# Expert and SwiGLU stage: two up products in a row, then the down products of both

## The chip, the cores and the metric

The program runs on one core of a Trainium2 chip. TensorE multiplies matrices into PSUM; VectorE (DVE), ScalarE (ACT) and GpSimd (POOL) do the element-wise work; SyncE (SP) issues the transfers. The metric is the device time of one execution in microseconds. Before the change three runs took 2143.82, 2144.63 and 2146.75 us, so the median is 2144.63.

## The reference

Attention with a local or a strided mask, a mixture of eight experts whose token weights come from Sinkhorn iterations, and a SwiGLU block with RMS norm, all in float32:

```
attn = softmax(where(mask, q k^T / sqrt(64), -1e9)) v          # 4 x 8 heads x 576 x 64
x    = attn as 2304 tokens x 512
P    = exp(x w_gate - max);  8 times: rows / sum, columns / sum, * N / E
moe  = sum over e of P[:, e] * (relu(x w1[e]) w2[e])           # 8 experts, 512 -> 1024 -> 512
xn   = moe / sqrt(mean(moe^2) + 1e-6) * rms_g
out  = (silu(xn w_gate2) * (xn w_val)) w_out                   # 512 -> 1536 -> 512
```

## The kernel before

Attention and expert 0 come first and take about 330 us of the span. The change lies in what follows: experts 1 to 7 and the SwiGLU block (three passes over its hidden columns, treated as groups 8 to 10). The tokens are cut in three thirds of 768. A *visit* is one group on one third; the list `quads` holds the 21 visits of experts and the 9 of SwiGLU in order.

A visit consists of *rounds*: four for an expert, two for a SwiGLU pass. Each matrix is split into a high and a low part, and a product of two such matrices is three matmuls (high by high, high by low, low by high). The up side uses a scheme of seven block products (`PROD`, line 839) in place of eight. One entry of `PROD` is a `product` (line 1016): six matmuls of 384 columns into one of two PSUM banks, `ub0` and `ub1`. The tuple's third number says which bank, the fourth whether the bank starts anew:

```
PROD = [(0, 0, 0, True), (1, 1, 1, True), (4, 4, 0, False), (3, 3, 1, True),
        (5, 5, 0, False), (6, 2, 1, False), (2, 6, 0, False)]
```

An expert round runs these seven once. A SwiGLU round runs them twice, for the gate and then for the value, fourteen products in all. The banks swap roles after each seven (`turn_u`).

`outcome(i, a, b, use)` (line 1041) issues what reads a product out. For products 0, 2 and 3 it is a ScalarE copy (line 1047). For products 1, 4 and 5 of an expert it is a VectorE addition (line 1062), then relu on ScalarE (line 1036) and on VectorE the low part of the hidden block (line 1037). For product 6 relu and the low part read the bank directly. SwiGLU has a sigmoid (1073) and multiplications (1074, 1084), with additions in 1071 and 1082. A bank may be written again only when its reader is done; a product that accumulates waits for that reader too.

A *down* (`down_one`, line 1437) is three matmuls of 512 columns (lines 701 to 703) from a hidden block of the round before into one of six PSUM banks `db0` to `db5`. A round has twelve of them (`downs`, line 1420). In the first round of a visit the downs of the visit before come to their end, and `evict` (line 1454) issues a VectorE instruction for each of the six banks (line 1460 for experts, 1471 for SwiGLU). Such a round is called an eviction round in what follows.

What decides the order: the loop over products (line 1558) issues a product, its outcome and one step of the background clock (`bg.pump`), then as many downs as the list `upto` (line 1514) allows after this product, each with a step of that clock. Each engine runs its instructions in the order of issue. Background work hangs on that clock: the conversion of the SwiGLU weights on VectorE (`convert`, lines 805 to 826), the splitting of the next weights (`combine`, lines 856 to 863, and `prepare_2`, lines 934 and 937 on ScalarE and GpSimd), loads and stores. Three rounds in which tiles are transposed for the norm take `upto` from the table `TURNS` (line 1492). In the first visit `columns_1` (line 687) writes column sums into the free part of a product bank, which line 691 reads.

Of the kernel before, what the change touches and what calls it, by code (L numbers as in the profile page):

```python
# [92 lines left out]
def kernel(  # L93
# [595 lines left out]
    def columns_2(area, ps):  # L689
        c = area[:, NTILE + E : NTILE + 2 * E]  # L690
        nc.vector.tensor_scalar(out=c, in0=ps, scalar1=1e-9, scalar2=None, op0=ALU.add)
        nc.vector.reciprocal(out=c, in_=c)
        nc.vector.tensor_tensor(
            out=prob, in0=prob, in1=c[:, None, :].to_broadcast([P, NTILE, E]), op=ALU.mult
        )
        nc.vector.tensor_scalar(out=prob, in0=prob, scalar1=float(NT) / E, scalar2=None, op0=ALU.mult)
# [467 lines left out]
    with tc.manual_schedule():  # L1164
# [117 lines left out]
        for g in range(1, len(groups)):  # L1282
            due = SL * (first[g] // TA) - 4 * (LOOK + (PRE if groups[g][0] else 0)) - DUE
            steps = [step for t in ticks[last[g - 1] + 1 : last[g] + 1] for step in t]
# [62 lines left out]
        for idx in range(-LOOK, n1 - LOOK):  # L1347
# [8 lines left out]
            if u.f == 0:  # L1356
                if "x" not in u.cell:
                    fetch(u)
                if u.left:
                    bg.add(gate(u.t0, u.n, u.cell["x"]), 20)  # L1360
                    if u.at:
                        area = fa[:, :1280], fa[:, 1280:3328].bitcast(F32R)
                        steps = sums(0, us[0].cell["x"], *area) if u.at == 1 else []
                        steps += sums(u.at, u.cell["x"], *area)
                        bg.add(steps, 30 if u.at == 1 else SUMS, tag="sums")
                else:
# [5 lines left out]
                    steps = []  # L1372
# [17 lines left out]
            if not u.left and u.f == 0:  # L1390
                begin_psum()
                place = db[4], db[5], acc[:, 0], wgc2
                steps = []
# [26 lines left out]
        def downs(r):  # L1420

            n, j, hs = r
            g, qd, _ = quads[n]
            last_j = NF // 2 - 1 if g < E else NG // 2 - 1
            half = NF // 2 if g < E else NG // 2
            order = (1, 2, 3, 0) if j == 0 else (0, 1, 2, 3)
            seen = set()
            out = []
            for i in order:
                f = j + (half if i in (2, 3) else 0)  # L1430
                for t in range(3):
                    b = t + (3 if i in (1, 2) else 0)
                    out.append((r, i, t, b, f, j == 0 and b not in seen, j == last_j and b in seen))
                    seen.add(b)
            return out
# [61 lines left out]
        for n, (g, qd, ends_group) in enumerate(quads):  # L1497
# [10 lines left out]
            for j in range(rounds):  # L1508
                chains = [j] if g < E else [2 * j, 2 * j + 1]
                steps = 7 * len(chains)  # L1510
                hs = [4 * ((hround + 1) % 2) + i for i in range(4)]
                hround += 1
                todo = downs(done) if done is not None else rest
                upto = [len(todo) * (i + 1) / steps for i in range(steps)]
                turns = {}
                if turning is not None:
                    at, upto = TURNS[steps]
# [31 lines left out]
                for ci, s in enumerate(chains):  # L1549
# [8 lines left out]
                    for i, (wk, xk, which, begins) in enumerate(PROD):  # L1558
# [16 lines left out]
                        if n == 0 and i in (1, 6):  # L1575
# [4 lines left out]
                            steps = [lambda to=free_part: columns_2(totals, to)]  # L1580
# [61 lines left out]
```

## Time and profile before

| | |
|---|---|
| median of three runs | 2144.63 us |
| the profiled execution | 2145.55 us, of which the span of instructions 2143.7 us |
| TensorE matmul | 2086.0 us, 97% of the span, 11343 matmuls |
| TensorE weight load | 1860.9 us, 87% |
| VectorE | 1198.2 us, 56% |
| ScalarE | 747.1 us, 35% |
| GpSimd | 211.6 us, 10% |
| granted TensorE clock | 9 tenths or more in all 40 slices |
| DMA | 149 GB/s in the mean |

The span is the time from the first to the last instruction of the profiled execution. Busy shares are means over stages. Matmuls are pipelined: the row of one lasts longer than the distance to the next, so distances are read from start to start. A wait view lists idle stretches of over 150 ns, by the instruction that ended them.

### The profile page before, as it was taken

The page shows a single profiled execution, that of the slowest core. Times are in us where ns is not written, and L with a number is a line of the kernel's source. Part 1 is how long each engine was busy: PE and PEld are TensorE (multiplying, and loading weights), DVE is VectorE, ACT ScalarE, POOL GpSimd, SP SyncE. Part 2 cuts the span into 40 slices and gives each one's busy share as a digit, 9 for nine tenths or more (in the row PEclk, how much of TensorE's full clock was granted, in tenths as well). Part 3 has the DMA queues.
Part 4 walks back from the last instruction along what each step waited for, and adds up shares of the span by engine and source line. Part 5 has one row for each costly group of instructions (what it writes and reads, how often), then busy time and mean ns, then how long its engine had stood idle before and what let it go on. Part 6 is the DMA issues. An engine that isn't in the chain of part 4 may idle for free.

```text
span 2143.7 us, 30671 instructions
## 1 busy us (share of the span) xinstructions
PE 2086.0 (97%) x11343; PEld 1860.9 (87%) x11343; DVE 1198.2 (56%) x2625; ACT 747.1 (35%) x1762; POOL 211.6 (10%) x231
## 2 busy tenths in 40 slices
PE   8999999999999999999999999999999899999999
PEld 7889888888888888888888888888887789888888
DVE  4567756657446644744564465455357565546544
ACT  7756333223223322322332232233334343423322
POOL 6322301101000100110010001001000000000000
PEclk9999999999999999999999999999999999999999
DMA  7576474544445264344525534441364673253342
GB/s 193 143 206 174 134 225 146 196 155 123 147 134 170 72 192 148 121 148 142 166 74 165 171 121 144 132 162 60 108 200 140 220 224 125 81 195 123 115 176 88
DMA packets 350756, 319.23 MB, mean 149 GB/s; under 512 B 88976, under 2 KB 274320, under 8 KB 350608
## 3 DMA queue, kind: packets, MB, share of 16 engines
q1 hardware_dynamic: 350608, 317.29, 47.4%
q8 instruction: 89, 1.46, 0.3%
q14 instruction: 59, 0.48, 0.1%
HBM read 237.78 MB, written 79.43 MB: 148 GB/s over the span
## 4 chain that ended last, share of the span: by engine, by line
PE 81%; DVE 10%; ACT 4%; DMA 3%; issue 2%; SPq 1%; POOL 0%; DVEq 0%; ACTq 0%
PE ub L1019 35%; PE db L702 12%; PE db L703 12%; PE db L701 11%; PE psh L701 1%; PE psh L703 1%; PE psh L702 1%; DVE cv L1084 1%; DVE acc L1460 1%; PE psy L701 1%; PE psy L702 1%; PE ps_s L471 1%; PE psy L703 1%; DVE cv L1082 1%; DMA fa<-in_moe_w_dram 1%
## 5 line engine op out<-in xcount | busy, mean ns | idle before, releaser
L1019 PE MATMUL ub<-xt,w1t 128*128 128x384 f32 x2000 | 495.0, 339 | 14.3 <-DVE cv L1082 3.6
L1019 PEld LDWEIGHTS ub<-xt,w1t 128*128 128x128 f32 x2000 | 366.1, 188 | 65.7 <-DVE cv L1084 8.2
L1019 PE MATMUL ub<-xx,w1t 128*128 128x384 f32 x1600 | 395.8, 340 | 10.6 <-DVE fa L1071 6.8
L1019 PEld LDWEIGHTS ub<-xx,w1t 128*128 128x128 f32 x1600 | 293.9, 189 | 48.4 <-DVE fa L1071 7.4
L1062 DVE TENSOR_TENSOR fa<-ub,fa 128x384 f32<-128x384 f32 x252 | 140.0, 556 | 299.8 <-PE ub L1019 298.7
L1047 ACT COPY fa<-ub 128x384 f32<-128x384 f32 x360 | 171.3, 476 | 343.5 <-PE ub L1019 343.4
L1019 PE MATMUL ub<-xt,w1x 128*128 128x384 f32 x808 | 272.2, 337 | 0.0
L703 PE MATMUL db<-w2t,ht 128*128 128x512 f32 x644 | 255.7, 397 | 0.0
L702 PE MATMUL db<-w2t,ht 128*128 128x512 f32 x644 | 254.8, 396 | 0.0
L701 PE MATMUL db<-w2t,ht 128*128 128x512 f32 x644 | 251.0, 390 | 0.0
L701 PE MATMUL db<-w2t,hx 128*128 128x512 f32 x612 | 242.0, 395 | 7.8 <-DVE acc L1114 5.2
L703 PE MATMUL db<-w2t,hx 128*128 128x512 f32 x612 | 244.8, 400 | 0.0
L702 PE MATMUL db<-w2t,hx 128*128 128x512 f32 x612 | 243.5, 398 | 0.9 <-POOL w2t L937 0.9
L937 POOL TENSOR_TENSOR w2t<-fa,w2t 128x512 fp32r<-128x512 f32 x68 | 90.8, 1336 | 1480.7 <-ACT w2t L934 1455.7
L1019 PE MATMUL ub<-xx,w1x 128*128 128x384 f32 x632 | 213.6, 338 | 0.0
L1036 ACT ACTIVATE hx<-fa 128x384 fp32r<-128x384 f32 x126 | 66.2, 526 | 265.4 <-DVE fa L1062 263.6
L1036 ACT ACTIVATE ht<-fa 128x384 fp32r<-128x384 f32 x126 | 66.2, 525 | 262.1 <-DVE fa L1062 262.1
L1019 PEld LDWEIGHTS ub<-xt,w1x 128*128 128x128 f32 x808 | 152.0, 188 | 0.0
L703 PEld LDWEIGHTS db<-w2t,ht 128*128 128x128 f32 x644 | 120.7, 187 | 26.1
L703 PEld LDWEIGHTS db<-w2t,hx 128*128 128x128 f32 x612 | 115.5, 189 | 26.6 <-DVE hx L1033 1.8
L701 PEld LDWEIGHTS db<-w2t,hx 128*128 128x128 f32 x612 | 115.9, 189 | 20.9 <-DVE acc L1114 7.0
L701 PEld LDWEIGHTS db<-w2t,ht 128*128 128x128 f32 x644 | 121.1, 188 | 11.0
(202 smaller groups left out, 2974.1 us busy)
## 6 DMA issues: line engine op xcount, KB each, us to landing
fa<-in_moe_w_dram SPq DMA_DIRECT2D x112, 256.0 KB
xt<-xdt SPq DMA_DIRECT2D x32, 768.0 KB
xx<-xdt SPq DMA_DIRECT2D x28, 768.0 KB
xt<-xnd SPq DMA_DIRECT2D x28, 768.0 KB
y1d<-acc SPq DMA_DIRECT2D x72, 256.0 KB
acc<-y1d SPq DMA_DIRECT2D x72, 256.0 KB
xx<-xnd SPq DMA_DIRECT2D x21, 768.0 KB
xt<-xdh SPq DMA_DIRECT2D x50, 192.0 KB
```

The lines of the kernel that those rows point to most:

```text
L471: nc.tensor.matmul(ps[:mq, i * nk : (i + 1) * nk], z[:, n, :, :].rearrange("p h c -> p (h c)"), t[:, c0 : c0 + nk], start=True, stop=True,)
L701: nc.tensor.matmul(ps, lh, rh, start=first, stop=False)
L702: nc.tensor.matmul(ps, lh, rl, start=False, stop=False)
L703: nc.tensor.matmul(ps, ll, rh, start=False, stop=last)
L937: nc.gpsimd.tensor_sub(out=w2t[:, i, 1], in0=t, in1=w2t[:, i, 0].bitcast(F32))
L1019: nc.tensor.matmul(ps[:, :TH], w[i][:, c], x[:, k, c], start=first and c == 0 and n == 0, stop=c == 1 and n == 2, skip_group_check=True,)
L1036: nc.scalar.activation(h[0], src, AF.Relu)
L1047: nc.scalar.copy(keep[(0, None, 1, 2)[i]], b if i == 3 else a)
L1062: nc.vector.tensor_tensor(out=src, in0=ps, in1=more, op=ALU.add)
L1082: nc.vector.tensor_tensor(out=to, in0=ps, in1=more, op=ALU.add)
L1084: nc.vector.tensor_tensor(out=to, in0=src, in1=scratch(n), op=ALU.mult)
L1460: nc.vector.scalar_tensor_tensor(out=a, in0=db[b], scalar=prob[:, ti, g : g + 1], in1=a, op0=ALU.mult, op1=ALU.add)
```

## The change

One line changes: the list that says how many downs may have been issued after product i. It was proportional to the products done. Now it is 0 after products 0, 2, 4 and so on, except the last one of a round, and unchanged after the others.

```
-                upto = [len(todo) * (i + 1) / steps for i in range(steps)]
+                upto = [len(todo) * (i + 1) / steps if i % 2 or i == steps - 1 else 0 for i in range(steps)]
```

With twelve downs and seven products (an expert round), the downs issued behind products 0 to 6 were 2, 2, 2, 1, 2, 2, 1 and are now 0, 4, 0, 3, 0, 4, 1. With fourteen products (a SwiGLU round) they were one behind each product but 6 and 13, and are now 2, 2, 2, 1, 2, 2, 1 behind products 1, 3, 5, 7, 9, 11, 13. Rounds that take `upto` from `TURNS` are as before.

On TensorE, at the end of the first round of the second visit of expert 4 (the last matmul of product 6, then product 0 of the next round, which is one row of six matmuls, then what follows), the order before is:

```order
L1019 MATMUL ub0_4208<-xx_3857,w1x_3856 128x384
L701 MATMUL db2_3962<-w2t_78,ht_80 128x512
L702 MATMUL db2_3962<-w2t_78,ht_80 128x512
L703 MATMUL db2_3962<-w2t_78,ht_80 128x512
L1019 MATMUL ub1_4209<-xt_79,w1t_77 128x384 x6
L701 MATMUL db3_3963<-w2t_78,hx_3858 128x512
L702 MATMUL db3_3963<-w2t_78,hx_3858 128x512
L703 MATMUL db3_3963<-w2t_78,hx_3858 128x512
L701 MATMUL db4_3964<-w2t_78,hx_3858 128x512
L702 MATMUL db4_3964<-w2t_78,hx_3858 128x512
L703 MATMUL db4_3964<-w2t_78,hx_3858 128x512
L1019 MATMUL ub0_4208<-xt_79,w1t_77 128x384 x2
```

and after the change:

```order
L1019 MATMUL ub0_4208<-xx_3857,w1x_3856 128x384
L701 MATMUL db2_3962<-w2t_78,ht_80 128x512
L702 MATMUL db2_3962<-w2t_78,ht_80 128x512
L703 MATMUL db2_3962<-w2t_78,ht_80 128x512
L1019 MATMUL ub1_4209<-xt_79,w1t_77 128x384 x6
L1019 MATMUL ub0_4208<-xt_79,w1t_77 128x384 x2
L1019 MATMUL ub0_4208<-xt_79,w1x_3856 128x384
L1019 MATMUL ub0_4208<-xt_79,w1t_77 128x384 x2
L1019 MATMUL ub0_4208<-xt_79,w1x_3856 128x384
L701 MATMUL db3_3963<-w2t_78,hx_3858 128x512
```

`ub1` is written by product 0, `ub0` by product 6 and product 1, `db2` to `db4` by downs. Product 1 has moved ahead of the two downs behind product 0.

On VectorE in the same round, from the first of the six evictions (line 1460) to the last, before:

```order
L1460 SCALAR_TENSOR_TENSOR acc_3855<-db3_3963,prob_75,acc_3855 128x512
L1062 TENSOR_TENSOR fa_81<-ub0_4208,fa_81 128x384
L1037 SCALAR_TENSOR_TENSOR hx_3858<-fa_81,hx_3858 128x384
L1460 SCALAR_TENSOR_TENSOR acc_3855<-db4_3964,prob_75,acc_3855 128x512
L1460 SCALAR_TENSOR_TENSOR acc_3855<-db5_3965,prob_75,acc_3855 128x512
L1062 TENSOR_TENSOR fa_81<-ub1_4209,fa_81 128x384
L1037 SCALAR_TENSOR_TENSOR hx_3858<-fa_81,hx_3858 128x384
L1460 SCALAR_TENSOR_TENSOR acc_3855<-db0_3960,prob_75,acc_3855 128x512
L1460 SCALAR_TENSOR_TENSOR acc_3855<-db1_3961,prob_75,acc_3855 128x512
L1037 SCALAR_TENSOR_TENSOR hx_3858<-ub0_4208,hx_3858 128x384
L1460 SCALAR_TENSOR_TENSOR acc_3855<-db2_3962,prob_75,acc_3855 128x512
```

and after:

```order
L1460 SCALAR_TENSOR_TENSOR acc_3855<-db3_3963,prob_75,acc_3855 128x512
L1062 TENSOR_TENSOR fa_81<-ub0_4208,fa_81 128x384
L1037 SCALAR_TENSOR_TENSOR hx_3858<-fa_81,hx_3858 128x384
L1062 TENSOR_TENSOR fa_81<-ub1_4209,fa_81 128x384
L1037 SCALAR_TENSOR_TENSOR hx_3858<-fa_81,hx_3858 128x384
L1460 SCALAR_TENSOR_TENSOR acc_3855<-db4_3964,prob_75,acc_3855 128x512
L1460 SCALAR_TENSOR_TENSOR acc_3855<-db5_3965,prob_75,acc_3855 128x512
L1460 SCALAR_TENSOR_TENSOR acc_3855<-db0_3960,prob_75,acc_3855 128x512
L1460 SCALAR_TENSOR_TENSOR acc_3855<-db1_3961,prob_75,acc_3855 128x512
L1037 SCALAR_TENSOR_TENSOR hx_3858<-ub0_4208,hx_3858 128x384
L1460 SCALAR_TENSOR_TENSOR acc_3855<-db2_3962,prob_75,acc_3855 128x512
```

The rows of 1062 and 1037 that name `ub0` and `ub1` are the outcomes of products 4, 5 and (1037 reading `ub0` directly) 6. The second and third eviction have moved from ahead of outcome 5 to behind it; what stands ahead of outcome 6 is the same set.

## Rows read from the trace of the kernel before

**Rows 1.** The page's busy line: busy us (share of span) x instructions, by engine.
```profile
PE 2086.0 (97%) x11343; PEld 1860.9 (87%) x11343; DVE 1198.2 (56%) x2625; ACT 747.1 (35%) x1762; POOL 211.6 (10%) x231
```

**Rows 2.** TensorE's waits: who, for whom: us in total, times, longest us.
```profile
PE ub L1019 <- DVE hx L1037: 3.2, 7, 0.7
```

**Rows 3.** Timeline, an ordinary expert round: start us, us, engine, line, operation, tiles, count, [idle].
```profile
772.16 0.39 PE L701 MATMUL db<-w2t,hx 128*128 128x512 f32 x1
...
772.86 0.39 PE L701 MATMUL db<-w2t,hx 128*128 128x512 f32 x1
...
773.55 0.51 PE L1019 MATMUL ub<-xt,w1t 128*128 128x384 f32 x2
...
774.60 0.39 PE L701 MATMUL db<-w2t,hx 128*128 128x512 f32 x1
...
775.32 0.56 DVE L1037 SCALAR_TENSOR_TENSOR ht<-ub,ht 128x384 fp32r<-128x384 f32 x1 [1.25 <-ACT ht L1036]
...
776.36 0.39 PE L701 MATMUL db<-w2t,ht 128*128 128x512 f32 x1
```

**Rows 4.** Timeline, two of four downs in a row at 325 us.
```profile
324.92 0.39 PE L701 MATMUL db<-w2t,ht 128*128 128x512 f32 x1
...
325.60 0.39 PE L701 MATMUL db<-w2t,ht 128*128 128x512 f32 x1
```

**Rows 5.** Timeline, the end of a SwiGLU visit at 1928 to 1937 us.
```profile
1931.54 0.55 DVE L1082 TENSOR_TENSOR cv<-ub,fa 128x384 f32<-128x384 f32 x1
...
1932.58 1.20 PE L1019 MATMUL ub<-xt,w1t 128*128 128x384 f32 x6
...
1933.62 0.39 PE L701 MATMUL db<-w2t,ht 128*128 128x512 f32 x1
...
1933.93 0.56 DVE L1084 TENSOR_TENSOR cv<-ub,fa 128x384 f32<-128x384 f32 x1
...
1936.42 0.51 PE L1019 MATMUL ub<-xx,w1t 128*128 128x384 f32 x2
```

**Rows 6.** Timeline, a light eviction round at 975 to 982 us.
```profile
975.16 0.56 DVE L1062 TENSOR_TENSOR fa<-ub,fa 128x384 f32<-128x384 f32 x1 [0.38 <-PE ub L1019]
...
976.31 0.56 DVE L1037 SCALAR_TENSOR_TENSOR hx<-fa,hx 128x384 fp32r<-128x384 f32 x1 [0.59 <-ACT hx L1036]
...
976.79 1.40 DVE L1460 SCALAR_TENSOR_TENSOR acc<-db,prob,acc 128x512 f32<-128x512 f32 x2
...
979.72 1.41 DVE L1460 SCALAR_TENSOR_TENSOR acc<-db,prob,acc 128x512 f32<-128x512 f32 x2
...
981.04 0.55 DVE L1037 SCALAR_TENSOR_TENSOR hx<-ub,hx 128x384 fp32r<-128x384 f32 x1
...
981.52 0.39 PE L701 MATMUL db<-w2t,hx 128*128 128x512 f32 x1
```

**Rows 7.** Timeline, a heavy eviction round at 601 to 605 us.
```profile
602.19 1.22 PE L1019 MATMUL ub<-xx,w1t 128*128 128x384 f32 x6
...
603.25 0.39 PE L701 MATMUL db<-w2t,hx 128*128 128x512 f32 x1
...
604.48 0.55 DVE L1037 SCALAR_TENSOR_TENSOR hx<-ub,hx 128x384 fp32r<-128x384 f32 x1
...
605.09 0.44 PE L1019 MATMUL ub<-xt,w1t 128*128 128x384 f32 x1 [0.29 <-DVE hx L1037]
```

**Rows 8.** Timeline, a middle eviction round at 729 to 731 us.
```profile
729.29 0.39 PE L701 MATMUL db<-w2t,hx 128*128 128x512 f32 x1
...
729.90 0.55 DVE L1037 SCALAR_TENSOR_TENSOR hx<-ub,hx 128x384 fp32r<-128x384 f32 x1
```

**Rows 9.** Timeline, the first visit's column sum at 370 us.
```profile
369.98 0.40 PE L701 MATMUL db<-w2t,ht 128*128 128x512 f32 x1
...
370.13 0.16 DVE L691 TENSOR_SCALAR cv<-ub 128x8 f32<-128x8 f32 x1
```

**Rows 10.** Timeline, VectorE's outcome 6 in the last visit of expert 7.
```profile
1660.67 0.55 DVE L1037 SCALAR_TENSOR_TENSOR hx<-ub,hx 128x384 fp32r<-128x384 f32 x1
```

## Prediction

> **What bounds the kernel now.** I read the busy line of the page first, then TensorE's waits by whom it waited for, then the timeline at the ends of rounds. TensorE works 97% of the span [rows 1], so a microsecond counts only if TensorE issues its matmuls closer together or stands still for longer. It hardly stands still now: among the expert rounds its largest repeated wait is the one for line 1037, the low part of a hidden block on VectorE, 3.2 us in seven pieces [rows 2]. The reader is to see two things. First, the stream is full, so the change can win only by the matmuls' spacing. Second, its one weak place is the first `product` of a round that needs a PSUM bank which VectorE has not yet read out.
>
> Words used: a round has products 0 to 6 (SwiGLU: 0 to 13) and twelve downs (one down is three 512-column matmuls); "outcome k" is what ScalarE and VectorE do with product k. Products use two banks in turn, so a product waits for an outcome two or three products back. A visit is one expert (or SwiGLU pass) on one third of the tokens. 84 expert rounds and 18 SwiGLU rounds exist; three rounds that turn tiles take their table from TURNS and keep their order, so 82 and 17 change.
>
> **Part 1: which distances change.** Before, an expert round runs its downs in groups of 2,2,2,1,2,2,1 behind products 0 to 6; now 0,4,0,3,0,4,1. I count what lies on TensorE between a product and the next user of its bank. For products 2, 3, 4, 5 and 6 the count is the same (product 2 after outcome 0: product 1 and four downs, both times). Product 0 of the next round gains two downs of distance from outcome 5. Product 1 of the next round loses two: from outcome 6 it had one down, product 0 and two downs, now one down and product 0. Two downs take 0.70 + 0.69 = 1.39 us [rows 3]. In SwiGLU the bank distances stay, except product 7 (one down more from outcome 5) and product 9 (one less from a single ScalarE copy, still a down and a product).
>
> So the new place of product 1 is, to the hundredth, where the first down behind product 0 stands today. That gives its lateness straight from the rows: end of the VectorE row of outcome 6, plus 0.06 us from there to a matmul's start (604.48 + 0.55 to 605.09 in [rows 7]), less the start of that down.
>
> Ordinary rounds (62 changed): 775.32 + 0.56 + 0.06 = 775.94 against 776.36 [rows 3]: 0.42 us to spare, cost nothing. ScalarE's relu and VectorE's subtraction fit into a down and a product. If this cover went, each 0.1 us would cost 6 us in all. Five of the 62 have VectorE behind by the same reading: four by 0.46, 0.46, 0.27 and 0.35, and one (row at 1660.67, [rows 10]) where product 1 already starts as soon as outcome 6 is done and so loses both downs, 1.39. Sum 2.9.
>
> Eviction rounds (the first round of a visit, 20 times), in which VectorE also empties the six down banks of the visit before, 0.70 us each (1.41 for two, [rows 6]):
> - Light, 7 of 20: 981.04 + 0.55 + 0.06 - 981.52 = 0.13 late [rows 6]; the seven, 0.13 to 0.21, sum 1.1.
> - Middle, 6 of 20: 729.90 + 0.55 + 0.06 - 729.29 = 1.22 [rows 8]; the six lie between 0.48 and 1.23, sum 4.8.
> - Heavy, 7 of 20: product 1 waits already, 605.09 instead of 603.25 + 1.39 = 604.64; it would now be wanted at 603.25 [rows 7]. It starts when it did, with two downs fewer behind it: 1.39 each, sum 9.7.
>
> This takes outcome 6 to end when it does today. The order of VectorE changes: two evictions move from before outcome 5 to behind it. From outcome 4's addition at 975.16 to outcome 6 at 981.04 VectorE rests only for ScalarE, 0.59 us per outcome [rows 6], and the same instructions stand between those two points in both orders. A saturated queue ends at the same time in any order, if nothing comes later than its turn. Outcomes 4 and 5 take VectorE 1.63 each (975.16 to 976.79), to 978.4; the evictions' turns come at 978.4, 979.1, 979.7 and 980.4. Product 5 and its four downs (part 2: 1.04 + 2.75) end 3.8 behind product 4, about 978.7, so the third and fourth are ready and the first two long are. Bounds: from 1.0 less in a round (one VectorE row that ran long beside a GpSimd subtraction may escape it) to two evictions, 1.4, more where VectorE wasn't saturated; I take 0, since the rows show it saturated, plus 0.04 each because product 6 comes that much sooner (3.79 behind product 4, not 3.83): 0.8 in all. Eviction rounds together: 1.1 + 4.8 + 9.7 + 0.8 = 16.4.
>
> The first visit has Sinkhorn's column sums in the free part of a product bank. Product 3 overwrites beside them and now follows product 2 at once: wanted at 369.98, but VectorE reads the sum at 370.13 to 370.29 [rows 9], so 0.37 late; two rounds like it, one without, one that loses a down: 1.5.
>
> **Part 2: spacing.** The time of a down depends on its neighbours: 0.70 behind a product, 0.69 before one [rows 3], 0.68 between two downs [rows 4]. A product takes 1.06 behind a single down [rows 7], 1.05 behind two [rows 3], 1.04 behind a product [rows 5]. An expert round before: 7 x 0.70 + 5 x 0.69 + 2 x 1.06 + 5 x 1.05 = 15.72; now 4 x 0.70 + 5 x 0.68 + 3 x 0.69 + 1.06 + 3 x 1.05 + 3 x 1.04 = 15.60. That is -0.12 x 82 = -9.8 us. A SwiGLU round: downs -0.05, products from 12 x 1.06 + 2 x 1.04 to 2 x 1.06 + 5 x 1.05 + 7 x 1.04, -0.15; -0.20 x 17 = -3.4. Its last products wait for VectorE's chain anyway: outcome 12 begins at 1931.54, outcome 13's product is read until 1934.49, product 2 follows at 1936.42 [rows 5]. With two downs instead of one ahead of product 12 and none between 0 and 1, the same additions give 1936.4 to 1936.5. So only what is won before product 11 stays, about half: -1.7. Bounds for both: 0 (the rows come from short runs) and -13.2.
>
> Here the Trainium skill ("TensorE: Matmul & The Clock Gate", Back-to-back issue gap) has a rule that says more: a warm stream issues one matmul per N / 2.4 + 2.5 ns, by which a down would take 0.65 and a product 0.975. The trace doesn't get there: downs in a run of four take 0.68 [rows 4]. If the lengthened runs did reach it, 5 x 0.03 + 3 x 0.065 more would go per expert round, some 28 us in all, and the time would be about 2126.
>
> **Sum.** 16.4 + 2.9 + 1.5 - 9.8 - 1.7 = +9.3 us. On the profiled execution, 2145.55 (its span 2143.7 and 1.85 around it), that is 2154.9. The median of the runs is 0.92 lower than that execution, so 2154.
>
> What moves with the order and costs nothing: the background steps are clocked by products and downs alike, nineteen per expert round, so conversions, weight loads, SP's queue and GpSimd's subtractions keep their place to within two of the nineteen; a down is issued at the same or a later step, so no weight is needed sooner.
>
> **Rivals.**
> 1. The runs repay the wait. If every down in a changed expert round came at 0.68 and every product at 1.04, a round would take 15.44, 0.28 less than today: -23 us, -1.7 for SwiGLU, against the same 20.8 of waits: 2140.7 by the median, and anything up to 2148.9 if part of it holds or if the heavy rounds come out lighter. For it: both figures exist in the trace. Against it: the first and last member of a run are dearer, and doubling leaves four first and three last ones. This is the case that is not slower. The skill's rule above would be this mechanism carried further; of the chance below, 0.02 is for that.
> 2. The burst costs more. Four evictions in a row stand directly ahead of outcome 6; where VectorE was not saturated they push it back by two evictions, 1.4 us, in the 13 light and middle rounds: +18, 2172. The gapless row of VectorE speaks against it; a plain round with more background work than the one I read speaks for it.
> 3. Spacing gains nothing, since weight loads and not neighbours set it: 2145.6 + 20.8 - 0.9 = 2165.
>
> **Chances.** Forecast (2149 to 2160 around it) 0.58; rival 3 and mixtures up to 2168 0.14; rival 2 0.06; rival 1 0.22, of which 0.18 within 0.2% and 0.04 beyond. 0.2% (4.3 us) is about what a measurement of this kernel can tell from no change. So slower 0.78, same 0.18, faster 0.04. The range 2146 to 2167 leaves out half of rival 1's faster end and rival 2.
>
> **What would show it.** TensorE's waits for line 1037 rise from seven, 3.2 us, to some seventeen pieces and 15 to 20 us, nearly all at the first matmul of product 1 in the second round of a visit. The heavy ones are about 2 us, the middle ones 0.5 to 1.1, and ordinary rounds show none. Downs inside a run of four take 0.68; the second of two products 1.04. SwiGLU's rounds keep their length within 0.2 us. I am wrong if ordinary rounds show waits (0.42 to spare was not enough), if the waits for line 1037 stay near 3 us, or if runs of four downs keep 0.695 each.

## The result and the profile after

The changed kernel takes 2172.45 us in the median of four runs (2169.54 to 2175.85), against 2144.82 in four runs of the kernel before (2143.82 to 2146.75): ratio 1.013, 95% interval 1.0115 to 1.0144. It is slower, as forecast, but by 27.6 us and not by 9.3, and 2172 lies above the range of 2146 to 2167. The profiled execution after took 2174.68 us, its span is 2172.6: 28.9 more than the span of 2143.7 before. Two runs of kernels below, at 2268.76 and 2962.73 us, had a granted clock of 0.85 and 0.65 in the mean; the ratios leave them out.

The page's busy line after, to be held against [rows 1]:

```profile
PE 2092.8 (96%) x11343; PEld 1870.9 (86%) x11343; DVE 1193.9 (55%) x2625; ACT 747.8 (34%) x1762; POOL 212.3 (10%) x231
```

The same matmuls are busy for 6.8 us longer in sum (2092.8 against 2086.0; part of it at a lower clock, below), where the forecast had them closer together. The other 22 of the 28.9 us are time in which TensorE stood. Its waits after (who, for whom: us in total, times, longest us):

```profile
PE ub L1019 <- DVE hx L1037: 16.9, 16, 2.2
PE ub L1019 <- DVE cv L1084: 9.7, 16, 1.1
...
PE db L1113 <- DVE acc L1104: 4.1, 3, 1.7
...
PE ub L687 <- DVE cv L684: 3.0, 2, 2.0
...
PE ub L1019 <- DMA xx<-xdt: 1.6, 2, 1.0
```

Line 1037 stood at 3.2 us in seven pieces [rows 2] and now at 16.9 in sixteen, as forecast. Two rows have no counterpart before: a matmul of Sinkhorn's column sums in the first visit (line 687) waits for line 684, and a token block is not loaded in time. Two others were shorter before:

```profile
PE ub L1019 <- DVE cv L1084: 4.4, 9, 0.6
...
PE db L1113 <- DVE acc L1104: 3.0, 3, 1.1
```

Line 1113 is the transposition of tiles for the norm, line 1104 the VectorE instruction that scales them. The view counts only stretches of over 150 ns, so the light rounds, where TensorE stands for less, do not show in it.

Two second rounds of a visit, as timeline rows (start us, us, engine, line, operation, tiles, count, [idle before]); the wait for outcome 6 of the eviction round stands at their start. A heavy one, the answer to [rows 7]:

```profile
607.87 1.23 PE L1019 MATMUL ub<-xx,w1t 128*128 128x384 f32 x6
...
609.50 0.74 DVE L1460 SCALAR_TENSOR_TENSOR acc<-db,prob,acc 128x512 f32<-128x512 f32 x1
610.16 0.55 DVE L1037 SCALAR_TENSOR_TENSOR hx<-ub,hx 128x384 fp32r<-128x384 f32 x1
...
610.76 0.62 PE L1019 MATMUL ub<-xt,w1t 128*128 128x384 f32 x2 [1.67 <-DVE hx L1037]
```

A middle one, the answer to [rows 8], with the four evictions that now stand in a row ahead of outcome 6:

```profile
734.73 2.72 DVE L1460 SCALAR_TENSOR_TENSOR acc<-db,prob,acc 128x512 f32<-128x512 f32 x4
...
737.37 0.54 DVE L1037 SCALAR_TENSOR_TENSOR hx<-ub,hx 128x384 fp32r<-128x384 f32 x1
...
737.97 0.61 PE L1019 MATMUL ub<-xx,w1t 128*128 128x384 f32 x2 [0.91 <-DVE hx L1037]
```

Measured from the first matmul of product 6 to that of the next product 6, where both orders have issued the same work, such rounds grew by 1.41 (the heavy one) and 1.17 us (the middle one); the prediction had 1.39 and 1.22. An ordinary round after, TensorE alone, to be read from start to start beside [rows 3] and [rows 4]:

```profile
784.05 1.22 PE L1019 MATMUL ub<-xt,w1t 128*128 128x384 f32 x6
785.12 0.51 PE L1019 MATMUL ub<-xx,w1t 128*128 128x384 f32 x2
...
786.15 0.39 PE L701 MATMUL db<-w2t,ht 128*128 128x512 f32 x1
786.85 0.39 PE L701 MATMUL db<-w2t,ht 128*128 128x512 f32 x1
787.54 0.39 PE L701 MATMUL db<-w2t,ht 128*128 128x512 f32 x1
788.24 0.39 PE L701 MATMUL db<-w2t,ht 128*128 128x512 f32 x1
788.92 0.51 PE L1019 MATMUL ub<-xx,w1t 128*128 128x384 f32 x2
...
789.98 0.51 PE L1019 MATMUL ub<-xx,w1t 128*128 128x384 f32 x2
...
791.02 0.39 PE L701 MATMUL db<-w2t,ht 128*128 128x512 f32 x1
```

The four downs take 0.70, 0.69, 0.70 and 0.68. The product behind them takes 1.06 (788.92 to 789.98), the one behind a product 1.04. Over all changed expert rounds the medians are 0.698, 0.691, 0.692, 0.680 for the downs and 1.066 and 1.040 for the products. So only the fourth down of a run is short, and the product behind a run is dearer than the 1.05 that stood behind two downs before. The changed ordinary rounds came out 0.007 us shorter, not 0.12.

**A cause that the sum did not hold.** In visit 8, one of the heavy ones, the second round grew by 2.93, not by 1.39. (Visits are counted from 0 in the order of `quads`: 0 to 20 are the experts', 21 to 29 SwiGLU's.) The windows from 855 us on show why (window, its length, then busy us of PE, PEld, DVE, ACT, POOL with instructions, then the granted clock, DMA share, GB/s):

```profile
855.00:867.60 12.60, 10.79 (x54) 9.51 (x53) 9.07 (x19) 2.78 (x6) 0.00 (x0) 1.00 0.30 109
867.60:871.00 3.40, 3.40 (x9) 2.65 (x8) 2.73 (x8) 1.07 (x3) 0.00 (x0) 0.50 0.48 146
871.00:886.00 15.00, 15.00 (x76) 13.54 (x75) 7.70 (x19) 5.03 (x12) 0.00 (x0) 1.00 0.58 191
```

From 867.6 to 871.0 the granted clock is 0.50, the lower level (1.2 GHz). Just before, TensorE had stood for line 1037:

```profile
866.25 0.62 PE L1019 MATMUL ub<-xt,w1t 128*128 128x384 f32 x2 [1.81 <-DVE hx L1037]
...
867.41 0.46 PE L701 MATMUL db<-w2t,hx 128*128 128x512 f32 x1
868.52 0.63 PE L701 MATMUL db<-w2t,hx 128*128 128x512 f32 x1
869.80 0.63 PE L701 MATMUL db<-w2t,hx 128*128 128x512 f32 x1
871.05 0.40 PE L701 MATMUL db<-w2t,hx 128*128 128x512 f32 x1
```

Downs at the lower level take 1.28 and 1.25 us instead of 0.69. The same happens at 1444.4, and in the first visit at 389.7 behind the new wait of line 687, whose row there is:

```profile
389.24 0.39 PE L687 MATMUL ub<-cv,ones 128*128 128x8 f32 x2 [1.97 <-DVE cv L684]
```

Further new stretches at 0.50 begin at 1686.8 (at the end of 2.23 us of standing for line 1037) and at 1987.2. Length times what the clock lacked, summed over all such stretches within the span, is 27.9 us after and 17.5 before. That is an upper bound of their price, since TensorE also waited within some of them.

Where the 28.9 us lie, by rounds from product 6 to product 6:

| rounds | difference, us |
|---|---|
| second rounds of the 18 expert visits n = 1 to 18 | +17.0, of which 3.1 by the two stretches at half clock |
| their other 54 rounds | +0.1 |
| first visit | +4.0, of which 1.5 by half clock |
| visits 19 to 21, around the normalisation | +6.0, of which 1.3 by half clock |
| SwiGLU, 16 rounds | +0.3 (first rounds -2.0, second rounds +2.3, of which 1.4 by half clock) |
| up to the first product 6, and the end | +1.5 |

The half-clock shares are read against the same rounds in traces without such a stretch there: 1.38 in the filled kernel (run 5) for visits 8 and 17, 1.04 and 1.77 in the second trace of the changed kernel (run 6) for the first visit and visit 20, 0.69 in runs keep1 and swiglu_only for the SwiGLU round.

### The profile page after: what moved, and what is told of

Its sections match the earlier page's. It is cut to its first block, busy times and chain, and to the rows that moved or that the text cites. A ratio compares the mean times of both kernels' runs of the same rounds, so it can differ in the third digit from the quotient of the medians.

```text
span 2172.6 us, 30658 instructions
## 1 busy us (share of the span) xinstructions
PE 2092.8 (96%) x11343; PEld 1870.9 (86%) x11343; DVE 1193.9 (55%) x2625; ACT 747.8 (34%) x1762; POOL 212.3 (10%) x231
## 4 chain that ended last, share of the span: by engine, by line
PE 78%; DVE 11%; ACT 4%; DMA 3%; issue 2%; SPq 0%; POOL 0%; DVEq 0%; ACTq 0%; POOLq 0%
PE ub L1019 34%; PE db L702 11%; PE db L703 11%; PE db L701 11%; DVE acc L1460 2%; PE psh L701 2%; PE psh L702 1%; PE psh L703 1%; DVE cv L1084 1%; PE psy L701 1%; PE ps_s L471 1%; PE psy L702 1%; DVE hx L1037 1%; PE psy L703 1%; DVE fa L1062 1%
```

## The experiments

Theory W: the loss is the wait for outcome 6, since two downs fewer stand between it and the next user of its bank, plus other waits of that kind in the first visit and in visits 19 to 21. Theory S: spacing brings nothing, because what some members of a run gain others lose. Theory K: waits of 2 us also bring the clock down. Each has its rival in what was expected. Differences of rounds are always against the kernel before, and of one profiled execution each. Edits are shown against the changed kernel (9 against the one before), with `...` for what is left out.

**1. Two downs, or one, between products 0 and 1 of the second rounds only.** Two undo the distance, one halves the loss. The second rounds of visits 19 and 20 take their list from `TURNS`, so the edit does not reach them.

```
  upto = [... if i % 2 or i == steps - 1 else 0 ...]
+ if j == 1 and g < E and n:
+     upto[0] = 2        # keep2; keep1 has 1
```

keep2:

> The changed kernel, but in the round behind an eviction round (20 expert rounds) two downs stay between product 0 and product 1. Theory W (product 1 waits for outcome 6, which stands behind four evictions): the waits for line 1037 fall back to about 4 us and the half-speed stretches of the clock at 868 and 1444 us go with them, 17 us less, about 2155. Rival U (a loss spread evenly over all changed rounds, by spacing or weight loads): only 20 of 99 rounds are touched, about 2167. Rival S (SwiGLU rounds carry the loss): 2172.

keep1:

> As keep2, with one down kept ahead of product 1. Theory W: each heavy round still loses one down (0.69), middle ones at most 0.5, light ones nothing, some 6 us of the 17 stay; waits end below 1.5 us each, and with them the half-speed stretches in these rounds: about 2159. Rival U: 2167 to 2170. Rival S: 2172.

keep2 took 2155.48 us (2151.58 to 2156.46), ratio 1.0046 (1.0031 to 1.0061); keep1 2161.65 (2160.86 to 2163.21), ratio 1.0079 (1.0064 to 1.0094). The waits for line 1037, of keep2 and then of keep1:

```profile
PE ub L1019 <- DVE hx L1037: 4.5, 8, 2.2
```
```profile
PE ub L1019 <- DVE hx L1037: 9.1, 12, 2.2
```

With two downs put back the heavy round of visit 4 waits 0.29 us, the very wait of before [rows 7], and the second rounds are 2.0 us shorter than before in sum. With one they are 4.5 longer: the heavy ones by 0.70 to 0.82, half of 1.41. By the times, 17 us (2172.45 less 2155.48) hang on these two downs. The rest of the change stays in keep2, runs of four and evictions in a row included, and is not faster: its expert rounds without a wait differ by 0.007 us. What remains in keep2's profiled execution (2151.58, the fastest of its four) is +2.9 in the first visit and +5.3 in visits 19 to 21. keep1 came out above the 2159 that was expected; its first visit lost 5.9 us, with the granted clock at 0.50 for 6.8 and for 3.4 us in it.

**2. Pairs in SwiGLU alone.**

```
- upto = [... if i % 2 or i == steps - 1 else 0 ...]
+ upto = [... if i % 2 or i == steps - 1 or steps == 7 else 0 ...]
```

> Pairs of products in SwiGLU rounds alone, expert rounds as before. Theory W: these rounds keep their length (bank distances are the same), 2143 to 2147. Rival S: about 2170. Prediction's spacing term, if it held: 2143.

2146.94 (2144.18 to 2148.37), ratio 1.0005 (0.9996 to 1.0015): no difference. The waits for line 1084, the end of VectorE's chain, rose from 4.4 to 10.2 us:

```profile
PE ub L1019 <- DVE cv L1084: 10.2, 16, 1.1
```

The first rounds are 1.4 us shorter, the second ones 1.2 longer. What is won early in a visit is waited for at its end.

**3. Pairs in visits 1 to 18 alone.**

```
+ pairs = g < E and 0 < n < 19
- upto = [... if i % 2 or i == steps - 1 else 0 ...]
+ upto = [... if not pairs or i % 2 or i == steps - 1 else 0 ...]
```

> Pairs in all rounds of the eighteen expert visits n = 1 to 18 only; the first visit, the visits 19 to 21 around the normalisation and the SwiGLU rounds keep the alternating order. Theory: the changed kernel's loss is the sum of parts that lie where the order is paired: about +17 in the second rounds of visits (with two clock falls in it), about 0 in other rounds, +4 in the first visit, +6 in visits 19 to 21. So here 2145 + 17 = 2162 and no loss in the first visit or in 19 to 21. Rival (the clock falls in the first visit and in 19 to 21 come from the runs of downs elsewhere, or fall about by chance): those visits stay 4 and 6 us longer, 2169 to 2172.

2161.18 (2159.11 to 2162.22), ratio 1.0073 (1.0058 to 1.0089). The second rounds are 14.0 us longer in the trace; the first visit is 0.4 shorter and visits 19 to 21 0.6. So the loss lies only where the order is paired; the other 11 us belong to the visits that keep the old order here. This trace has no stretch at half clock between 354 and 1651 us, although the waits of visits 8 and 17 are there; hence runs 5 to 7.

**4. Pairs in rounds without evictions alone**, so spacing by itself (`j > 1` added to the line of 3).

> Pairs only in the third and fourth rounds of the eighteen expert visits n = 1 to 18 (36 rounds), the alternating order everywhere else: rounds without evictions, in which product 1 has 0.42 us to spare, so spacing alone. Prediction's part 2: -0.12 us a round, 36 x 0.12 = -4.3, about 2140.8. Theory S (a product behind a run of downs takes 1.07 and the third down of a run 0.69, so what the inner ones gain the outer ones lose): the rounds come out within 0.02 us of the kernel before, and the time within 1 us of 2145.

2144.81 in the median of eleven runs, against 2146.13; ratio 0.9994 (0.9985 to 1.0003). The forecast's -4.3 us would be 0.998, outside the interval. Spacing is worth nothing that can be told from zero. The profiled execution of this kernel had a granted clock of 0.85 nearly throughout, so its rounds are compared with each other only; at full clock the same 36 rounds of the changed kernel differ from those before by 0.007 us in the median. An unchanged round and then a paired one, product 6 to product 6:

```profile
768.12:785.06 16.94, 16.94 (x80) 14.80 (x79) 8.40 (x19) 5.09 (x10) 2.58 (x2) 0.85 0.20 62
785.06:801.99 16.93, 16.93 (x79) 14.78 (x78) 6.58 (x15) 4.56 (x9) 2.58 (x2) 0.85 0.48 132
```

They differ by 0.01 us.

**5. The wait filled with work.** Six dummy matmuls between products 0 and 1 in the second rounds of visits 8 and 17, into a down bank that the next down begins anew.

```
+ if i == 0 and j == 1 and n in (8, 17):
+     (n0, j0, hs0), i0, t0, b0, f0, _, _ = todo[0]
+     x0, p0 = h_slot(hs0[i0])[0], w2_place(g, f0)
+     prep2.drain(("w2", p0))
+     for _ in range(6):
+         nc.tensor.matmul(db[b0], x0[:, t0 * P : (t0 + 1) * P], w2t[:, p0, 0], start=True, stop=True)
```

> The changed kernel with six 512-column matmuls put between product 0 and product 1 of the second round of two visits (n = 8 and 17), where product 1 waits about 2 us for the low part and where the changed kernel's trace shows a half-clock stretch of 3.4 us right behind the wait. The six write a down bank that the next down begins anew, so nothing of the result changes. Theory K (the clock falls because TensorE stood still): the two rounds are about 1.5 us shorter each (+1.4 over the kernel before in place of +2.93 and +2.98), product 1 starts when it did, and no stretch at half clock lies at either place. Rival (the clock falls there for another reason, or falls without regard to one wait): the half-clock stretches stay and the rounds keep +2.9. Time 2166 to 2172 by theory K, as the changed kernel (2169 to 2176) by the rival; the verdict is read from the two rounds, since 3 us is little against the run-to-run spread.

2173.95 (2170.32 to 2177.1), no less than the changed kernel: in the profiled execution the first visit lost 5.9 us in place of 4.0, with the clock at 0.50 for 10.2 us in it. The two rounds are 1.38 us longer than before in place of 2.93 and 2.98. Product 1 starts when it did, 3.05 behind product 0, and the clock stays up:

```profile
865.53 1.55 PE L1574 MATMUL db<-w2t,hx 128*128 128x512 f32 x6
...
867.52 0.61 PE L1019 MATMUL ub<-xt,w1t 128*128 128x384 f32 x2 [0.44 <-DVE hx L1037]
```
```profile
864.40:871.40 7.00, 6.56 (x31) 5.43 (x31) 6.20 (x15) 1.91 (x5) 0.00 (x0) 1.00 0.60 209
1441.00:1448.00 7.00, 6.56 (x32) 5.45 (x31) 6.23 (x16) 2.46 (x5) 0.00 (x0) 1.00 0.40 147
```

**6 and 7. The changed kernel and kernel 3 once more, unchanged**, one execution each, to see whether the stretches repeat.

> The changed kernel once more, one look. Open is whether the half-clock stretches of its trace belong to fixed places. Theory K (a 2 us stand of TensorE brings the fall): stretches of 3.4 us behind the waits of visits 8 and 17 again, as near 868 and 1444 us in the first trace. Rival (the fall needs more than the wait, since the kernel with pairs in visits 1 to 18 only has the same two waits and no stretch there): one or both are missing, and then the filled kernel without them shows less than it seems. Time 2169 to 2176.

> Pairs in visits 1 to 18 alone, a second look. The same question from the other side: the waits of visits 8 and 17 are there (1.98 us), its first trace has no half-clock stretch between 354 and 1651 us. Theory K: they appear now; rival: none, or one of the two. Time 2159 to 2163.

They took 2172.99 and 2166.37 us. In the repeated kernel 3 both stretches are there, where its first trace had none behind the same wait (first and second trace):

```profile
861.11 0.62 PE L1019 MATMUL ub<-xt,w1t 128*128 128x384 f32 x2 [1.82 <-DVE hx L1037]
```
```profile
862.50:867.00 4.50, 4.50 (x24) 4.03 (x23) 3.82 (x9) 2.11 (x5) 0.00 (x0) 1.00 0.44 132
```
```profile
867.05 0.62 PE L1019 MATMUL ub<-xt,w1t 128*128 128x384 f32 x2 [1.82 <-DVE hx L1037]
```
```profile
867.80:871.20 3.40, 3.40 (x11) 2.83 (x10) 2.30 (x7) 0.83 (x2) 0.00 (x0) 0.50 0.69 228
```

The changed kernel's second trace has the stretch in visit 17 and none in visit 8 or in the first visit. So of the eight waits of 1.81 or 1.82 us in these four traces, five are followed by half clock. Other long waits agree: the first visit's wait of 1.97 or 1.98 us for line 684 stands in seven traces of this record and is followed by half clock in four, and the 2.23 us wait of visit 20 ends in half clock in the changed kernel's first trace and not in its second. In none of these traces, nor in that of the filled kernel, does visit 1 to 18 hold such a stretch anywhere else. In these visits no fall came without such a wait, but the wait alone was not enough: theory K as it was put does not hold, and run 6's rival, that the fall needs more than the wait, does. Two filled waits without a fall agree with K, but at five in eight they could be luck. What else decides was not found.

**8. The evictions held back.** If VectorE's order is the cause, outcome 6 must come ahead of the evictions. The changed kernel, with the evictions behind products 4 and 5 (in SwiGLU 11 and 12) issued after the last outcome:

```
- if ends:
+ if ends and hold[0]:
+     held_out.append((n, b))
+ elif ends:
      evict(n, b)
...
  outcome(i, a, b, use)
+ hold[0] = ci == len(chains) - 1 and len(PROD) - 4 < i < len(PROD) - 1 and turning is None
+ if not hold[0]:
+     let_out()          # evict(*x) for all held
```

> The changed kernel, but evictions of the downs behind the last two products but one are issued on VectorE after the last outcome of the round instead of ahead of it; TensorE's order is that of the changed kernel. Theory W: outcome 6 ends up to 2.6 us earlier, the waits of product 1 for line 1037 all but vanish (those of the kernel before as well), SwiGLU's waits at products 0 and 1 shrink too: 2140 to 2150. Rival (the distance on TensorE alone decides, not what VectorE has ahead): 2172. Rival U: 2170.

2161.69 (2160.82 to 2162.12), ratio 1.0078 (1.0061 to 1.0094): the expectation missed. The second rounds did as expected (-2.6 us), and so did SwiGLU's (-5.4), but visits 19 to 21 lost 22 us: there the evicted tiles feed the normalisation. TensorE's waits show it; the first was 4.1 us in the changed kernel:

```profile
PE db L1113 <- DVE acc L1104: 9.0, 3, 4.6
...
PE db L1113 <- DVE acc L1469: 3.1, 1, 3.1
```

The second version holds nothing in visits 19 to 22 (`and not 18 < n < 23` in place of the last condition):

> The changed kernel with the evictions behind the last products but one held until the last outcome is issued, not in visits 19 to 22. In the first version with all evictions held, the second rounds of visits came out 2.6 us shorter than before and the SwiGLU rounds 5 us, and the normalisation lost 22. Theory W: without that loss the first visit (+4) and visits 19 to 21 (+6) stay, the second rounds are -2 to -3, SwiGLU -5: 2145 to 2150. Rival (the pairs cost where they stand, whatever VectorE does first): 2155 or more.

2149.01 in the median of ten runs, ratio 1.0012 (1.0002 to 1.0022). The second rounds come out 2.5 us shorter than before, SwiGLU 7.5, while the first visit (+6.0) and visits 19 to 21 (+6.4) keep their loss. So in the second rounds the pairs cost nothing once outcome 6 does not stand behind the evictions (the same hold in the kernel before gives -1.3, run 9).

**9. The same hold in the kernel before**, whose order on TensorE stays as it was.

> The kernel before, its order on TensorE unchanged, with VectorE's order changed: the evictions that fall behind the last two products but one are held and issued behind the last outcome of the round (not in visits 19 to 22, where the evicted tiles feed the normalisation). Theory W (what costs is that evictions stand ahead of outcome 6 on VectorE, which the change made dearer): the waits for the low part, 3.2 us in the kernel before, go nearly to nothing, and some of the 5 us that SwiGLU's second rounds wait for VectorE's chain go too: 2137 to 2142. Rival (the same VectorE work ahead of the following downs, which then wait for their banks): same as before, 2144 to 2147, with new waits of line 701 for the evictions.

2139.64 (2137.23 to 2143.0), ratio 0.9973 (0.9962 to 0.9984). Two second rounds, in visits 2 and 11, grew by 1.26 us each: five evictions had moved in front of the next round's outcomes. Without the hold there (`and n not in (2, 11)`):

> The kernel before with the same evictions held, not in visits 19 to 22 and not in visits 2 and 11, where holding them put five evictions into the next round and cost 1.26 us each: 2 x 1.26 = 2.5 us less than with these two, so 2137 against 2139.6 measured there and 2145 to 2146 of the kernel before. Rival (the 1.26 turns up in another round): 2139 to 2140 as there.

2138.02 (2136.16 to 2139.66), ratio 0.996 (0.9948 to 0.9973): 0.4% shorter than the kernel before, whose order on TensorE it has. Its second rounds are 3.8 us shorter than before, SwiGLU's 6.5. Outcome 6 now comes straight behind its relu, and four of the evictions behind it:

```profile
854.16 0.49 ACT L1036 ACTIVATE hx<-ub 128x384 fp32r<-128x384 f32 x1 [1.31 <-PE ub L1019]
...
854.81 0.55 DVE L1037 SCALAR_TENSOR_TENSOR hx<-ub,hx 128x384 fp32r<-128x384 f32 x1
855.27 2.71 DVE L1469 SCALAR_TENSOR_TENSOR acc<-db,prob,acc 128x512 f32<-128x512 f32 x4
```

## Why the prediction was right in sign and wrong in size

- **Part 1, waits in eviction rounds: right in visits 1 to 18.** Forecast 16.4 us for twenty rounds, some 15.9 of it in these visits. Measured are 17.0, or 13.9 without the 3.1 of half clock. Light rounds grew by 0.16 to 0.25, middle ones by 0.55 to 1.20, five heavy ones by 1.38 to 1.50 (the two with half clock taken from their filled version). Two heavy ones (visits 3 and 12) grew by 0.36 only: the bound "1.0 less in a round" came true there, since in visit 3 the row of line 806 beside a GpSimd subtraction takes 1.27 us before and 0.29 after. The other two rounds counted, in visits 19 and 20, take `TURNS` and keep their order; they grew by 0.63 and 0.59, also in keep2, and there the wait that grew is another, of line 1113 for line 1104 (1.08 us each before, 1.68 and 1.65 after). The four evictions in a row cost nothing more, so rival 2 failed as a mechanism, though its 2172 is the time that was measured. keep2 and keep1 tie the 17 us of visits 1 to 18 to the two downs. Of the five late ordinary rounds (2.9), two did not come at all (visits 3 and 12), two came at 0.30 and 0.44, and the fifth stands under visits 19 to 21.
- **Part 2, spacing: the step that failed.** -9.8 us were put down for the expert rounds; the rounds show -0.007 each, about -0.5 in all. The prices "0.68 for a down between two downs" and "1.05 for a product behind downs" were wrong for this stream. The 0.68 came from a run of four at 325 us [rows 4] in the stage before, where every down took 0.68; in an expert round only the fourth does. The run at 325 us follows up matmuls that have 512 columns as well, so no change of shape stands ahead of it (the row at 324.70 is line 703, `psh<-xt,w1t`, 128x512); whether that is the reason was not tried. A product behind three or four downs takes 1.066, not 1.05. Gains: 8.34 us of downs in a round become 8.30. Losses: 7.35 us of products (2 x 1.062 + 5 x 1.045) become 7.38. Run 4 shows it alone. This is rival 3's outcome, and it gave the waits without the spacing, 2165; its reason, the weight loads, was not tried. The rule weighed there is one that the Trainium skill ("TensorE: Matmul & The Clock Gate", Wait — 56ns, not 53.3ns?) states of back-to-back matmuls; the section named in the prediction has the same formula, but calls it the gap of a single matmul. It would give an estimate of 0.65 and 0.975; no down or product of an expert round after comes nearer than 0.68 and 1.04 in the medians, so this trace doesn't agree.
- **SwiGLU: a gain that was no gain.** Forecast -1.7 and its bound 0. Its first rounds win, its second rounds give much of it back in the wait for line 1084: 0.3 net, or -1.1 without the fall of the clock at 1987.2. Single rounds did not keep their length within 0.2 us: they moved by -1.4 to +0.75, and by 2.1 with the fall. Run 2 shows SwiGLU alone: no difference in time.
- **First visit: right kind, wrong place and size.** Forecast 1.5; measured 2.8 (second trace, no fall of the clock) and 4.0 (with one). The prediction looked at product 3, which overwrites beside the column sum, and overlooked that the column sum's own matmul, line 687, would stand for VectorE's line 684, for 1.00 and 1.97 us. Before, line 687 stood once, for line 1062 (0.93 us).
- **Visits 19 to 21: larger, +6.0 (7.9 in the second trace).** The late round at [rows 10] was put at 1.39 and came out at 1.77 (second trace), 3.06 with a fall of the clock. The first round of visit 20 was not in the sum at all: it grew by 2.1, with a wait of 1.6 for a token block's transfer (by 4.2 in the second trace, with a fall of the clock). What delays that transfer under the new order was not tried.
- **The clock: not in the sum.** About 7.3 of the 28.9 us: the five falls priced in the table. The forecast priced a wait at its own length.
- **Ordinary rounds** have no waits, as said: 0.42 us to spare was enough.

Put together, in us: the forecast of +9.3; 9.3 of spacing that never came; 7.3 of clock; 2.5 more in visits 19 to 21 (4.7 without the clock, against 2.2: the late round, 0.35 of an ordinary one and some 0.5 for two light ones); 1.5 outside the rounds; 1.0 in the first visit (2.5 against 1.5); 0.6 of SwiGLU; less 2.0 in the second rounds of visits 1 to 18 and 0.9 in their late ordinary rounds. That gives 28.6 against the 28.9 us between the two spans.

## What to carry to other kernels

The spacing of matmuls in a run must be read from a run of the same kind in the same loop, the first, the inner and the last member and the one that follows apart; where there is no such run, the gain of a reordering is better put at zero. A wait that the order adds is cheap to forecast from rows, at (end of the releasing instruction) minus (start of what stands in the new place today), and it should be searched for at every small matmul and every transfer that hangs on the same clock of steps. When a stream is full, look at what stands ahead of the releasing instruction on the other engine: moving up to four evictions behind one subtraction won 0.4% here, and neither order of TensorE that was tried won anything.

## What the runs showed of the hardware

- A wait of TensorE can cost more than its length. Behind five of eight waits of 1.8 us the granted clock was 0.50 for 3.4 us, and the round lost 1.5 us more. The fifteen waits of 1.67 to 1.75 us in visits 4, 9 and 13 of the same four traces and the filled kernel's had none behind them. What decides was not found. The same kernel had both falls in one execution and none in another: 2166.37 and 2159.11 us in these two profiled executions, of which the two falls explain 3.1 us. Another 5.8 lie ahead of the first visit, which began at 333.5 and 327.7 us, and SwiGLU's second rounds took 2.1 us less in the longer one.
- The stream does not scale with the granted clock. At 0.50, three 384-column matmuls take 0.96 us (390.39 to 391.35 below), at full clock 0.54 and 0.52, so 1.8 times and not twice as long. At 0.85 a round takes 16.93 us against 15.69: 1.08 times and not 1.18. So part of the spacing at full clock does not follow the granted clock; what sets it was not tried. (The 0.85 is of one trace, that of run 4.)

```profile
390.39 0.84 PE L1019 MATMUL ub<-xx,w1t 128*128 128x384 f32 x2
...
391.35 0.84 PE L1019 MATMUL ub<-xx,w1t 128*128 128x384 f32 x2
...
395.82 0.52 PE L1019 MATMUL ub<-xt,w1t 128*128 128x384 f32 x2
...
396.36 0.51 PE L1019 MATMUL ub<-xt,w1t 128*128 128x384 f32 x2
...
396.88 0.51 PE L1019 MATMUL ub<-xt,w1t 128*128 128x384 f32 x2
```
